# A second MLP whose first product is a one-level Strassen scheme on spans of 1024 tokens

## The chip, the cores and the metric

The kernel runs on one core of one Trainium2 chip. The metric is the device time of one execution in microseconds. The inputs and outputs are float32; the matrix products are made of pairs of float32r words, as told below.

## What is computed

Two steps of attention, then a gated MLP, then a second MLP without a gate. The change is in the second MLP. The reference, cut to that:

```python
def reference(**kwargs):
    attn_out = _attn_ref(...)                 # [8, 8, 576, 64]
    x = attn_out.transpose(0, 2, 1, 3).reshape(4608, 512)
    x = _moe_ref(x=x, ...)                    # gated MLP, 512 -> 1536 -> 512
    return _moe2_ref(x=x, ...)

def _moe2_ref(x, w_in, w_out):                # x [4608, 512]
    h = x @ w_in                              # w_in [512, 2048]
    g = h * (1.0 / (1.0 + np.exp(-1.702 * h)))
    return (g @ w_out).astype(np.float32)     # w_out [2048, 512]
```

The weights reach the kernel as pairs of 32-bit words, from which it builds float32 values on the chip.

## The kernel before

**Splitting.** Every operand of a large product is split into a float32r part h and a float32r rest l, and a product is three matmuls, h·h, h·l and l·h. A 512-deep product of a 128-row block thus takes 4 x 3 = 12 matmuls.

**The first MLP** (`mlp1`) runs in four units of two batches, 12 steps of 128 features each; attention of the next unit is woven into it, a stage at a time, by the driver loop at the end. `prods` multiplies weights with the packed attention values, `gateval` makes gate and value, `project` the output, which is summed in SBUF (`acc`) and written to DRAM (`x2_d`) as the second MLP's input. TensorE's results go through five PSUM buffers (pool `mm`); ACT, DVE and POOL empty them.

**Conversion.** `convert` turns one raw block of 128x512 word pairs into the two parts: an Abs on ACT, four bit operations on DVE (lines 116 to 119, with a buffer `between` in PSUM while the first MLP runs), a copy on ACT and a subtraction on POOL. The first MLP's weights are 36 such blocks, the second's 32.

**The second MLP** (`mlp2`). `early` runs beside the last unit of the first MLP: it converts nine of the sixteen 128-feature blocks of `w_in2` and `w_out2`, keeps three in SBUF and writes six to DRAM, and prepares the first tile of x. `main` then takes nine tiles of 512 tokens, and in each the sixteen feature blocks: `up(t, f)` makes 12 matmuls of 128x512 into one of four PSUM buffers, ACT applies the gelu, DVE splits the result (lines 903, 904); `down(t, f)` runs two blocks later and makes 4 x 3 matmuls of 128x512 that accumulate in four PSUM banks over all sixteen blocks, emptied once a tile. The remaining blocks are loaded and converted beside the first tile; from then on all weights lie in SBUF.

**Order.** The program is written in the order of its generators, and a scheduler with its own time model then orders the instructions of each engine; SP issues nearly all DMAs, in order. The stretches named below: attention and the first MLP up to 916 us, the second MLP from 916 us to the end.

## Time and profile before

| | |
|---|---|
| median of 3 runs | 1716.48 us (1715.28 to 1719.35) |
| span of the profiled execution | 1715.8 us |
| TensorE busy | 1686.7 us (98%) |
| VectorE (DVE), ScalarE (ACT), GpSimd (POOL) busy | 884.1, 677.0, 506.6 us |
| first matmul of the second MLP | 916.39 us |
| read from and written to DRAM | 138.41 and 44.04 MB |

The page's time is its span, from the first to the last instruction of one execution; the median of the runs is 0.7 us above it. A matmul's row has its modelled length, longer than the step from one start to the next, since matmuls are pipelined: the pace is read from starts. PEld is the load of the stationary operand, which overlaps matmuls.

### The profile page before, as it was taken

What the parts mean: (1) busy time and instruction counts of PE and PEld (TensorE: products, weight loads), DVE (VectorE), ACT (ScalarE), POOL (GpSimd) and SP (SyncE); (2) the same over time, 40 slices, a digit from 0 to 9 for tenths busy, and PEclk for the clock granted to TensorE, in tenths of its full rate; (3) what the DMA queues carried; (4) which work ended last, traced back from release to release, by engine and by line L of the source; (5) the groups of instructions that cost most, each with busy time, mean ns of one, the idle gap of its engine ahead of it and who ended that gap; (6) DMA issues with size and microseconds to landing.
All of it is one profiled execution on the core that took longest, in us unless ns stands there. A gap on an engine that the chain in (4) does not pass through costs nothing.

```text
span 1715.8 us, 24557 instructions
## 1 busy us (share of the span) xinstructions
PE 1686.7 (98%) x9360; PEld 1493.8 (87%) x9360; DVE 884.1 (52%) x1778; ACT 677.0 (39%) x1489; POOL 506.6 (30%) x515
## 2 busy tenths in 40 slices
PE   7899999999999999999999999999999999999999
PEld 5699998999999999999998888888888888888887
DVE  6789988657666566678884542212222222222221
ACT  5677776555555555555653321111111111110111
POOL 2357877544554355444662200000000000000000
PEclk9999999999999999999999999999999999999999
DMA  9666755543425443365666220101010101000000
GB/s 262 164 173 192 204 167 198 174 143 130 143 88 174 143 131 112 104 210 209 216 215 252 89 71 1 50 0 50 0 50 0 50 0 50 0 25 1 17 9 25
DMA packets 151909, 184.05 MB, mean 107 GB/s; under 512 B 87024, under 2 KB 123888, under 8 KB 144880
## 3 DMA queue, kind: packets, MB, share of 16 engines
q1 hardware_dynamic: 151504, 181.96, 33.5%
q8 instruction: 74, 1.21, 0.3%
q10 hardware_dynamic: 288, 0.52, 0.1%
q14 instruction: 43, 0.35, 0.1%
HBM read 138.41 MB, written 44.04 MB: 106 GB/s over the span
## 4 chain that ended last, share of the span: by engine, by line
PE 90%; DVE 3%; DMA 2%; ACT 2%; POOL 1%; SPq 1%; issue 1%; POOLq 0%; ACTq 0%; DVEq 0%
PE ps_up L897 23%; PE ps_dn L916 23%; PE ps_o L721 16%; PE ps_g L690 15%; PE ps_w L657 3%; PE ps_at L288 3%; PE ps_at L333 2%; PE ps_at L277 2%; PE ps_at L421 2%; DMA vn<-in_v_dram 1%; SPq L163 1%; DVE Wl L662 1%; PE ps_at L321 0%; POOL Hl L707 0%; DVE between L116 0%
## 5 line engine op out<-in xcount | busy, mean ns | idle before, releaser
L897 PE MATMUL ps_up<-xh,wi 128*128 128x512 f32 x1152 | 380.7, 393 | 0.7 <-DVE acc L731 0.7
L916 PE MATMUL ps_dn<-wo,gh 128*128 128x512 f32 x1152 | 356.5, 391 | 0.0
L903 DVE CAST gh<-gf 128x512 fp32r<-128x512 f32 x144 | 61.5, 427 | 514.3 <-ACT gf L900 508.9
L900 ACT ACTIVATE gf<-ps_up 128x512 f32<-128x512 f32 x144 | 86.2, 599 | 605.0 <-PE ps_up L897 586.2
L721 PE MATMUL ps_o<-Hh,wo 128*128 128x384 f32 x1152 | 323.1, 340 | 1.7 <-ACT Hh L706 1.2
L897 PEld LDWEIGHTS ps_up<-xh,wi 128*128 128x128 f32 x1152 | 216.2, 188 | 50.3 <-issue 1.0
L916 PEld LDWEIGHTS ps_dn<-wo,gh 128*128 128x128 f32 x1152 | 216.2, 188 | 47.9
L690 PE MATMUL ps_g<-Aqh,Wh 128*128 128x288 f32 x768 | 233.3, 304 | 4.1 <-ACT add L734 1.4
L690 PE MATMUL ps_g<-Aql,Wh 128*128 128x288 f32 x768 | 226.1, 295 | 0.0
L897 PE MATMUL ps_up<-xl,wi 128*128 128x512 f32 x576 | 225.8, 392 | 0.0
L690 PE MATMUL ps_g<-Aqh,Wl 128*128 128x288 f32 x768 | 225.5, 295 | 0.0
L916 PE MATMUL ps_dn<-wo,gl 128*128 128x512 f32 x576 | 224.4, 391 | 0.0
L721 PEld LDWEIGHTS ps_o<-Hh,wo 128*128 128x128 f32 x1152 | 210.7, 189 | 5.4 <-ACT Hh L706 1.9
L721 PE MATMUL ps_o<-Hl,wo 128*128 128x384 f32 x576 | 194.6, 339 | 1.1 <-POOL Hl L707 1.0
L707 POOL TENSOR_TENSOR Hl<-th,Hh 128x576 fp32r<-128x576 f32 x96 | 137.3, 1431 | 157.8 <-ACT Hh L706 155.9
L662 DVE TENSOR_TENSOR Wl<-ps_w,Wh 64x512 fp32r<-64x512 f32 x192 | 131.8, 687 | 71.9 <-ACT Wh L661 69.1
L736 POOL TENSOR_TENSOR acc<-acc,add 128x384 f32<-128x384 f32 x135 | 136.5, 1022 | 74.2 <-ACT add L734 72.2
L690 PEld LDWEIGHTS ps_g<-Aqh,Wh 128*128 128x128 f32 x768 | 144.0, 188 | 9.8 <-ACT add L734 1.6
L661 ACT CAST Wh<-ps_w 64x512 fp32r<-64x512 f32 x192 | 111.6, 581 | 83.2 <-PE ps_w L657 59.3
L690 PEld LDWEIGHTS ps_g<-Aql,Wh 128*128 128x128 f32 x768 | 144.3, 188 | 0.0
L690 PEld LDWEIGHTS ps_g<-Aqh,Wl 128*128 128x128 f32 x768 | 143.9, 188 | 0.0
L916 PEld LDWEIGHTS ps_dn<-wo,gl 128*128 128x128 f32 x576 | 108.1, 188 | 24.7
(154 smaller groups left out, 2506.9 us busy)
## 6 DMA issues: line engine op xcount, KB each, us to landing
wg<-wg SPq DMA_DIRECT2D x48, 1024.0 KB, 5.3
wo<-wo SPq DMA_DIRECT2D x48, 512.0 KB, 4.1
raw<-in_moe_w_out_dram SPq DMA_DIRECT2D x28, 512.0 KB, 4.0
x<-acc SPq DMA_DIRECT2D x32, 288.0 KB, 2.7
out_dram<-ob SPq DMA_DIRECT2D x34, 256.0 KB, 2.1
vn<-in_v_dram SPq DMA_DIRECT2D x16, 512.0 KB, 6.6
qn<-in_q_dram SPq DMA_DIRECT2D x64, 128.0 KB, 5.2
raw<-in_moe_w_in_dram SPq DMA_DIRECT2D x16, 512.0 KB, 3.8
```

The costliest lines, as they stand in the source:

```text
L288: nc.tensor.matmul(ps, x[:, a], y[:, a, span(e)], start=n == 0, stop=n == len(todo) - 1)
L657: last = nc.tensor.matmul(ps[:, a], st[:, i], mv[:, i], start=n == 0, stop=n == 2)
L661: nc.scalar.copy(Wh[rows, :, g], src)
L662: nc.vector.tensor_sub(Wl[rows, :, g], src, fl(Wh[rows, :, g]))
L690: nc.tensor.matmul(ps, st[:, o, g, c * P : (c + 1) * P], mv[:, g, cols], start=n == 0, stop=n == 3 * NG - 1)
L707: nc.gpsimd.tensor_sub(Hl, th, fl(Hh))
L721: nc.tensor.matmul(ps, st[:, m * P : (m + 1) * P], mv[:, cols], start=n == 0, stop=n == 3 * len(ss) - 1)
L736: nc.gpsimd.tensor_add(a, a, t)
L897: nc.tensor.matmul(ps, st[:, i], mv[:, i], start=n == 0, stop=n == 3 * NM - 1)
L900: nc.scalar.activation(gf, ps, AF.Gelu_apprx_sigmoid)
L903: nc.vector.tensor_copy(gh, gf)
L916: nc.tensor.matmul(pacc[r], st[:, r * P : (r + 1) * P], mv, start=f == 0 and n == 0, stop=f == NF2 - 1 and n == 2,)
```

## The change

The first product of the second MLP works on spans of 1024 tokens (four, and a last one of 512) and on pairs of feature blocks. A span's x is four quarters: b11 and b21 are the first and the second half of the depth for the first 512 tokens, b12 and b22 for the second 512. A pair's weights are four blocks a11 to a22. Instead of the eight block products there are seven, of sums and differences of blocks (`blocks`, `moving`); each is 2 x 3 = 6 matmuls, so a unit of one pair and one span has 42 of them and, with the second product, 90. In the last span they have 256 columns. The results are combined on DVE from four PSUM banks, one buffer each (`up`), with three products accumulated onto banks that already hold one.

The second product (`down`) no longer accumulates over the feature blocks in PSUM: for each pair and each 128 tokens six matmuls go to one of four banks, and DVE adds the bank to an accumulator in SBUF (`acc`; ACT copies it for the first pair).

All weights of the second MLP are converted during the first MLP once its own are done (`weights`, a step each 4.3 us of planned matmul time), with the sums of blocks formed and split there, and written to DRAM (`wi2_d`, `wo2_d`). `main` loads 1.8 MB (`wi`, two buffers) and 1.0 MB (`wo`, three buffers) for each pair and span, in alternating order of the pairs, so that the pair at a turn is kept. The first pair's blocks are loaded into the conversion buffers (`first_w`). x of the first span is prepared during the last unit of the first MLP (`first_x`), later spans during the last pair of the span before (`prepare`).

```diff
-    NKEPT = 3
-    NEARLY = 6
     MMB = 5
-    NTT = NT // TT
+    NP2 = NF2 // 2
+    TH = 512
+    WHOLE = NT // (2 * TH)
+    spans = [(i * 2 * TH, TH) for i in range(WHOLE)]
+    if NT % (2 * TH):
+        spans.append((WHOLE * 2 * TH, NT % (2 * TH) // 2))
+    SECOND = 4300.0
...
+    wi2_d = [dram.tile([P, 7, 2, 2, P], F32, name=f"wi2_{p}") for p in range(NP2)]
+    wo2_d = [dram.tile([P, 2, 2, DM], F32, name=f"wo2_{p}") for p in range(NP2)]
...
+        blocks = "s1 s2 s4 s3 a11 a12 a22".split()
+        moving = {"a11": "b11", "a12": "b21", "s4": "b22", "a22": "t4", "s1": "t1", "s2": "t2", "s3": "t3"}
...
+        def weights(banks):
+            for p in range(NP2):
+                ws = []
+                for h in range(2):
+                    r = raw_tile()
+                    nc.sync.dma_start(
+                        r.rearrange("p (i f) t -> p i f t", f=2 * P),
+                        w_in2[2 * h * P : 2 * (h + 1) * P, 2 * p * P : 2 * (p + 1) * P].rearrange(
+                            "(i p) f t -> p i f t", p=P
+                        ),
+                    )
+                    yield
+                    w = words(cv, r, DM, banks())
+                    ws.append(fl(w).rearrange("p (k i f) -> p i k f", k=2, f=P))
...
+                sums = cv.tile([P, 2, 2, 2, P], F32, tag="raw", name="sums", bufs=RAWS)
+                s1, s2, s4, s3 = (sums[:, i, j] for i in range(2) for j in range(2))
+                nc.gpsimd.tensor_add(s1, a21, a22)
+                nc.vector.tensor_sub(s3, a11, a21)
+                nc.vector.tensor_sub(s2, s1, a11)
+                nc.vector.tensor_sub(s4, a12, s2)
+                yield
+                for i in range(2):
+                    t = stage()
+                    nc.scalar.copy(t[:, :, 0], sums[:, i])
+                    nc.gpsimd.tensor_sub(t[:, :, 1], sums[:, i], fl(t[:, :, 0]))
+                    nc.sync.dma_start(wi2_d[p][:, 2 * i : 2 * i + 2], fl(t))
...
+                for f in range(2):
+                    r = raw_tile()
+                    nc.sync.dma_start(r, w_out2[(2 * p + f) * P : (2 * p + f + 1) * P])
+                    yield
+                    w = fl(words(cv, r, DM, banks()))
+                    t = cv.tile([P, 2, DM], F32R, tag="raw", name="stage", bufs=RAWS)
+                    nc.scalar.copy(t[:, 0], w)
+                    nc.gpsimd.tensor_sub(t[:, 1], w, fl(t[:, 0]))
+                    nc.sync.dma_start(wo2_d[p][:, f], fl(t))
...
-        def up(t, f):
-            xh, xl, _ = xt[t]
-            ih, il = wi[f]
-            ps = pools["pm"].tile([P, TT], F32, tag="up", name="ps_up")
-            n = 0
-            for i in range(NM):
-                for st, mv in ((ih, xh), (ih, xl), (il, xh)):
-                    nc.tensor.matmul(ps, st[:, i], mv[:, i], start=n == 0, stop=n == 3 * NM - 1)
-                    n += 1
-            gf = pools["sp"].tile([P, TT], F32, tag="gf", name="gf", bufs=2)
-            nc.scalar.activation(gf, ps, AF.Gelu_apprx_sigmoid)
-            gh = pools["sp"].tile([P, TT], F32R, tag="gh", name="gh", bufs=3)
-            gl = pools["sp"].tile([P, TT], F32R, tag="gl", name="gl", bufs=3)
-            nc.vector.tensor_copy(gh, gf)
-            nc.vector.tensor_sub(gl, gf, fl(gh))
-            gs[t, f] = gh, gl
...
-        def down(t, f):
-            gh, gl = gs.pop((t, f))
-            oh, ol = wo[f]
-            for r in range(TT // P):
-                if f == 0:
-                    pacc[r] = pools["pa"].tile([P, DM], F32, tag=f"dn{r}", name=f"ps_dn{r}")
-                for n, (st, mv) in enumerate(((gh, oh), (gh, ol), (gl, oh))):
-                    nc.tensor.matmul(
-                        pacc[r],
-                        st[:, r * P : (r + 1) * P],
-                        mv,
-                        start=f == 0 and n == 0,
-                        stop=f == NF2 - 1 and n == 2,
-                    )
-                if f == NF2 - 1:
...
+        def first_w():
+            t = [stage(), stage(), stage(), cv.tile([P, 1, 2, 2, P], F32R, tag="w", name="stage1", bufs=2)]
+            for i, x in enumerate(t):
+                nc.sync.dma_start(fl(x), wi2_d[0][:, 2 * i : 2 * i + x.shape[1]])
+            wi[0] = {q: t[i // 2][:, i % 2] for i, q in enumerate(blocks)}
...
+            def load_wi(n):
+                if n < len(seq) and seq[n][1] not in wi:
+                    p = seq[n][1]
+                    t = wp.tile([P, 7, 2, 2, P], F32R, tag="wi", name="wi", bufs=2)
+                    nc.sync.dma_start(fl(t), wi2_d[p])
+                    wi[p] = {q: t[:, i] for i, q in enumerate(blocks)}
...
+            def prepare(s, q):
+
+                if s == len(spans):
+                    return
+                n = spans[s][1]
+                b11, b12, b21, b22 = (xr[x] for x in ("b11", "b12", "b21", "b22"))
+                if q == "t2":
+                    xr[q] = spare()[:, :, :n]
+                    nc.vector.tensor_sub(xr[q], b22, b11)
+                source = {"t1": "b11", "t3": "b12", "t4": "b21"}.get(q, q)
+                split_x(q, xr[source], nc.gpsimd if q in ("b11", "b21", "b22") else nc.vector, n)
+                if q == "b11":
+                    nc.vector.tensor_sub(b11, b12, b11)
+                    nc.vector.tensor_sub(b12, b22, b12)
+                elif q == "b21":
+                    nc.vector.tensor_sub(b21, b21, xr["t2"])
...
+                def product(a, b, go_on=False):
+                    if not go_on:
+                        bank[b] = pm.tile([P, TH], F32, tag=f"up{b}", name="ps_up", bufs=1)[:, :n]
+                    wt, x, c = w[a], xb[moving[a]], 0
+                    for k in range(2):
+                        for y, z in ((0, 0), (0, 1), (1, 0)):
+                            nc.tensor.matmul(
+                                bank[b], wt[:, y, k], x[:, z, k], start=c == 0 and not go_on, stop=c == 5, skip_group_check=go_on
+                            )
+                            c += 1
+                    if last:
+                        prepare(s + 1, moving[a])
...
+                product("a11", 1)
+                p1 = temp("p1")
+                nc.scalar.copy(p1, bank[1])
                 yield
...
+                product("s2", 6)
+                u2 = temp("u2")
+                nc.vector.tensor_add(u2, p1, bank[6])
+                yield
+                product("s1", 5)
+                v5 = temp("v5")
+                nc.vector.tensor_add(v5, u2, bank[5])
+                yield
+                product("s3", 7)
+                c = temp("gf", 4)
+                nc.vector.tensor_add(c, v5, bank[7])
+                gelu(c, c, idx, 1, 1, n, nc.gpsimd)
+                yield
+                product("a12", 1, True)
+                gelu(temp("gf", 4), bank[1], idx, 0, 0, n, nc.gpsimd)
+                yield
+                product("s4", 5, True)
+                c = temp("gf", 4)
+                nc.vector.tensor_add(c, u2, bank[5])
+                gelu(c, c, idx, 0, 1, n, nc.gpsimd)
+                yield
+                product("a22", 7, True)
+                c = temp("gf", 4)
+                nc.vector.tensor_add(c, u2, bank[7])
+                gelu(c, c, idx, 1, 0, n, nc.vector)
+                yield
+
+            def gelu(gf, src, idx, i, k, n, engine):
+                nc.scalar.activation(gf, src, AF.Gelu_apprx_sigmoid)
+                gh, gl = (sp.tile([P, TH], F32R, tag=f"g{x}", name=f"g{x}", bufs=8)[:, :n] for x in "hl")
+                nc.vector.tensor_copy(gh, gf)
+                engine.tensor_sub(gl, gf, fl(gh))
+                g[idx, i, k] = gh, gl
...
+                for k in (1, 0):
+                    for r in range(per):
+                        ps = pa.tile([P, DM], F32, tag="dn", name="ps_dn", bufs=4)
+                        c = 0
+                        for i in range(2):
+                            gh, gl = g[idx, i, k]
+                            for st, y in ((gh, 0), (gh, 1), (gl, 0)):
+                                nc.tensor.matmul(
+                                    ps, st[:, r * P : (r + 1) * P], w[:, i, y], start=c == 0, stop=c == 5
+                                )
+                                c += 1
+                        m = k * per + r
+                        if first:
+                            acc[m] = sp.tile([P, DM], F32, tag=f"acc{m}", name="acc2", bufs=1)
+                            nc.scalar.copy(acc[m], ps)
+                        else:
+                            nc.vector.tensor_add(acc[m], acc[m], ps)
+                        if last:
+                            at0 = t0 + m * P
+                            nc.sync.dma_start(out[at0 : at0 + P, :], acc[m])
...
+            for idx, (s, p) in enumerate(seq):
+                ups = up(idx)
+                for _ in ups:
+                    next(behind_, None)
+                for _ in behind_:
+                    pass
+                nxt = [q for _, q in seq[idx + 1 : idx + 2]]
+                if idx and seq[idx - 1][1] not in (p, *nxt):
+                    wo.pop(seq[idx - 1][1], None)
+                if p not in nxt:
+                    wi.pop(p)
+                load_wi(idx + 2)
+                load_wo(idx + 2)
+                if idx and seq[idx - 1][0] != s:
+                    load_x(s + 1)
+                behind_ = down(idx)
...
+                    if finished():
+                        ready += what
+                        while ready >= SECOND:
+                            ready -= SECOND
+                            next(converting, None)
+            for _ in (*ahead, *converting):
                 pass
+            first_w()
```

TensorE in the middle of the second MLP. Before, `up` and `down` of one 512-token tile alternate (xh and xl are the parts of x, gh and gl those of the gelu's result):

```order
L897 MATMUL ps_up<-xh,wi_11814 128x512 x2
L897 MATMUL ps_up<-xl,wi_11814 128x512
L897 MATMUL ps_up<-xh,wi_11814 128x512
L916 MATMUL ps_dn_11887<-wo_11778,gh 128x512 x2
L916 MATMUL ps_dn_11887<-wo_11778,gl 128x512
L916 MATMUL ps_dn_11891<-wo_11778,gh 128x512 x2
L916 MATMUL ps_dn_11891<-wo_11778,gl 128x512
```

and now, where x_t and x_b are the seven moving operands and each product is six matmuls in a row:

```order
L999 MATMUL ps_up<-x_t_10160,wi 128x512 x6
L1062 MATMUL ps_dn<-wo_12819,gh 128x512 x2
L1062 MATMUL ps_dn<-wo_12819,gl 128x512
L1062 MATMUL ps_dn<-wo_12819,gh 128x512 x2
L1062 MATMUL ps_dn<-wo_12819,gl 128x512
L999 MATMUL ps_up<-x_b_10171,wi 128x512 x6
L1062 MATMUL ps_dn<-wo_12819,gh 128x512 x2
L1062 MATMUL ps_dn<-wo_12819,gl 128x512
```

Each block of the second product now ends after six matmuls, and its bank is emptied before it is used again.

DVE in the first MLP, where attention of a later unit is woven in. Before (Wl, kTl, acc and m are evictions of the first MLP and of attention):

```order
L662 TENSOR_TENSOR Wl<-ps_w,Wh 64x2x256
L402 STREAM_TRANSPOSE AT_4115<-t_4512 128x576
L662 TENSOR_TENSOR Wl<-ps_w,Wh 64x2x256
L144 TENSOR_TENSOR kTl<-ps_at,kTh 128x320
L728 COPY acc_4560<-ps_o 128x384
L662 TENSOR_TENSOR Wl<-ps_w,Wh 64x2x256
L728 COPY acc_4560<-ps_o 128x384 x2
L298 TENSOR_REDUCE m<-ps_at 128x1
L662 TENSOR_TENSOR Wl<-ps_w,Wh 64x2x256
```

and now, with the four operations of one conversion (raw_4565 is the block of word pairs):

```order
L119 TENSOR_SCALAR between<-w 128x512
L413 STREAM_TRANSPOSE AT_4148<-t_4563 128x576
L673 TENSOR_TENSOR Wl<-ps_w,Wh 64x2x256
L120 TENSOR_SCALAR between<-between 128x512
L155 TENSOR_TENSOR kTl<-ps_at,kTh 128x256
L739 COPY acc_4613<-ps_o 128x384
L155 TENSOR_TENSOR kTl<-ps_at,kTh 128x320
L121 SCALAR_TENSOR_TENSOR between<-raw_4565,between 128x512
L739 COPY acc_4613<-ps_o 128x384
L673 TENSOR_TENSOR Wl<-ps_w,Wh 64x2x256
L739 COPY acc_4613<-ps_o 128x384
```

The conversion's operations stand between the evictions, and the buffer `between` is held over them.

DVE at a turn from one token tile (before) or span (now) to the next. Before, one group splits the next x, and two banks of `down` are copied there by DVE:

```order
L903 CAST gh<-gf 128x512
L904 TENSOR_TENSOR gl<-gf,gh 128x512
L825 TENSOR_TENSOR xl<-xf,xh 128x512 x4
L903 CAST gh<-gf 128x512
L904 TENSOR_TENSOR gl<-gf,gh 128x512
L925 COPY ob<-ps_dn_12533 128x512
L903 CAST gh<-gf 128x512
```

and now, where u, v and gf are sums of product banks, xr the raw quarters of the next x, and x_t its split parts:

```order
L1071 TENSOR_TENSOR acc_12241<-acc_12241,ps_dn 128x512
L1015 TENSOR_TENSOR u_13145<-p_13123,ps_up 128x512
L978 TENSOR_TENSOR xr<-xr 128x1024
L1071 TENSOR_TENSOR acc_12259<-acc_12259,ps_dn 128x512
L979 TENSOR_TENSOR xr<-xr 128x1024
L974 TENSOR_TENSOR spare<-xr 128x1024
L1019 TENSOR_TENSOR v_13165<-u_13145,ps_up 128x512
L896 TENSOR_TENSOR x_t_13162<-xr,x_t_13162 128x1024
L1071 TENSOR_TENSOR acc_12277<-acc_12277,ps_dn 128x512
L1023 TENSOR_TENSOR gf<-v_13165,ps_up 128x512
L896 TENSOR_TENSOR x_t_13142<-spare,x_t_13142 128x1024
L1071 TENSOR_TENSOR acc_12300<-acc_12300,ps_dn 128x512
```

The eight subtractions of 1024 columns for the next span stand between the additions that empty TensorE's banks; five of them are seen here.

## Rows read from the trace of the kernel before

**Rows 1.** The page's busy line: us, share of the span, instructions.

```profile
PE 1686.7 (98%) x9360; PEld 1493.8 (87%) x9360; DVE 884.1 (52%) x1778; ACT 677.0 (39%) x1489; POOL 506.6 (30%) x515
```

**Rows 2.** The page's chain of work that ended last, by line.

```profile
PE ps_up L897 23%; PE ps_dn L916 23%; PE ps_o L721 16%; PE ps_g L690 15%; PE ps_w L657 3%; PE ps_at L288 3%; PE ps_at L333 2%; PE ps_at L277 2%; PE ps_at L421 2%; DMA vn<-in_v_dram 1%; SPq L163 1%; DVE Wl L662 1%; PE ps_at L321 0%; POOL Hl L707 0%; DVE between L116 0%
```

**Rows 3.** Stretches: busy us of PE, PEld, DVE, ACT, POOL; clock; DMA share; GB/s.

```profile
200.00:320.00 120.00, 116.14 (x778) 110.35 (x779) 95.11 (x199) 78.90 (x182) 82.86 (x83) 0.99 0.57 183
320.00:760.00 440.00, 440.00 (x3040) 427.97 (x3040) 287.63 (x615) 243.52 (x575) 212.21 (x219) 1.00 0.44 140
760.00:916.00 156.00, 154.00 (x1021) 150.66 (x1019) 121.68 (x224) 89.80 (x175) 87.34 (x72) 1.00 0.58 201
```

**Rows 4.** Costliest groups of the page: busy us, mean ns, idle before and releaser.

```profile
L897 PE MATMUL ps_up<-xh,wi 128*128 128x512 f32 x1152 | 380.7, 393 | 0.7 <-DVE acc L731 0.7
L900 ACT ACTIVATE gf<-ps_up 128x512 f32<-128x512 f32 x144 | 86.2, 599 | 605.0 <-PE ps_up L897 586.2
L897 PEld LDWEIGHTS ps_up<-xh,wi 128*128 128x128 f32 x1152 | 216.2, 188 | 50.3 <-issue 1.0
```

**Rows 5.** The chain in order of time: start us, us, what.

```profile
916.39 10.77 PE ps_up L897 x46
927.16 2.80 PE ps_dn L916 x12
...
1148.65 2.80 PE ps_up L897 x12
...
1703.43 8.21 PE ps_dn L916 x36
```

**Rows 6.** The timeline of TensorE, 256-column matmuls of attention: start us, modelled us.

```profile
479.77 0.28 PE L333 MATMUL ps_at<-vh,aTl 128*128 128x256 f32 x1
479.89 0.28 PE L333 MATMUL ps_at<-vh,aTh 128*128 128x256 f32 x1
```

**Rows 7.** DVE's groups by shape, from 916 us on, then before 916 us.

```profile
L904 DVE TENSOR_TENSOR gl<-gf,gh 128x512 fp32r<-128x512 f32 x144 | 99.5, 692 | 14.1 <-DVE gh L903 0.5
L903 DVE CAST gh<-gf 128x512 fp32r<-128x512 f32 x144 | 61.5, 427 | 514.3 <-ACT gf L900 508.9 <-PE ps_dn L916 5.3
L825 DVE TENSOR_TENSOR xl<-xf,xh 128x512 fp32r<-128x512 f32 x32 | 20.5, 702 | 3.5 <-ACT xh L824 3.5
...
L118 DVE SCALAR_TENSOR_TENSOR between<-raw,between 128x512 int32<-128x512 int32 x54 | 37.0, 686 | 0.4
L674 DVE TENSOR_TENSOR Aql<-AT,Aqh 128x576 fp32r<-128x576 f32 x16 | 13.0, 834 | 0.8 <-ACT Aqh L673 0.6
```

**Rows 8.** POOL's groups by shape, whole span.

```profile
L121 POOL TENSOR_TENSOR wo<-w,wo 128x512 fp32r<-128x512 f32 x22 | 28.4, 1291 | 58.2 <-ACT wo L120 58.2
L235 POOL TENSOR_TENSOR vl<-vn,vh 128x1024 fp32r<-128x1024 f32 x12 | 28.8, 2403 | 13.6 <-ACT vh L232 10.4 <-DMA qn<-in_q_dram 3.2
```

**Rows 9.** Waits of TensorE from 760 to 916: us in total, times, longest.

```profile
PE ps_g L690 <- DVE th L700: 0.5, 1, 0.5
PE ps_o L721 <- ACT add L734: 0.2, 1, 0.2
```

**Rows 10.** The timeline where the second MLP begins.

```profile
916.39 0.47 PE L897 MATMUL ps_up<-xh,wi 128*128 128x512 f32 x1 [0.74 <-DVE acc L731]
...
918.48 0.32 SPq L944 DMA_DIRECT2D wi<-w  x1
918.51 0.62 ACT L120 CAST wi<-w 128x512 fp32r<-128x512 f32 x1 [5.40 <-DMA x<-acc]
```

**Rows 11.** DMA of 918 to 938 in 40 slices; loads, KB each, us to landing.

```profile
GB/s 0 0 57 188 229 115 270 377 410 426 361 319 295 369 434 426 352 336 393 426 410 410 426 451 393 401 393 418 426 410 418 401 434 401 410 399 331 329 347 347
...
wi<-w SPq DMA_DIRECT2D x6, 512.0 KB, 9.2
...
wg<-wg SPq DMA_DIRECT2D x48, 1024.0 KB, 5.3
```

**Rows 12.** The timeline at the end: the last store's issue.

```profile
1712.28 0.34 ACTq L926 DMA_DIRECT2D out_dram<-ob  x1
```

More of the change, by code (lines that the diff above doesn't have):

```diff
@@ L1025, in tile_pack_attention__then__two_mlps @@
             u, ahead = 0, None
+            sources = [mm]
+            between = lambda: sources[-1]
+            weights, first_x, first_w, second = mlp2(cv)
+            converting, ready = weights(between), 0.0
             every = EVERY / len(todo)
```

249 lines of the change are left out of this document (129 added, 120 removed).

## The prediction

> **What bounds the kernel now.** I read the busy shares first: TensorE is busy 98% of the span [rows 1], and the chain that ended last is TensorE almost throughout, the two products of the second MLP alone 46% of it [rows 2]. Then the stretches [rows 3], all at full granted clock (2.4 GHz): of the 440 us from 320 to 760 TensorE idles none, of 200 to 320 it idles 3.9 us, of 760 to 916 2.0 us. A busy TensorE can hide slow issue, so I took its pace from the chain in order of time [rows 5]: twelve 512-column matmuls take 2.80 us at 927, where weights are converted and loaded beside them, and as long at 1148, where nothing else runs. From 916.39 to 1703.43 + 8.21 = 1711.64 lie 9 tiles x 16 x 24 = 3456 matmuls, so one costs 795.25 / 3456 = 0.2301 us, with no gap worth a term. So time is gained only by fewer or shorter matmuls, and lost only where TensorE is made to wait.
>
> **The matmuls removed.** The second product keeps its count: 36 blocks of 128 tokens x 8 pairs x 6 = 1728, all of 512 columns, as before. The first had 1728. Now four spans of 1024 tokens x 8 pairs x 42 = 1344 have 512 columns, and the last span (512 tokens) has 8 x 42 = 336 of 256 columns. Matmuls of 128x256 with a fresh 128x128 load each start 0.12 us apart [rows 6]. So 384 x 0.2301 = 88.4 us go and 336 x 0.12 = 40.3 us come: **-48.1 us**, all on the path, since the pace does not depend on what the other engines do [rows 5]. The Trainium skill (TensorE: Matmul & The Clock Gate, Back-to-back issue gap) gives a lone warm matmul N / 2.4 + 2.5 ns, thus an estimated 216 and 109 ns; by these the term would be 384 x 0.216 - 336 x 0.109 = 46 us. The same section's sustained 131 ns at 512 columns would make the 384 matmuls worth 50 us instead of 88. The rows agree with neither (2.80 us for twelve), so the trace decides.
>
> **More conversion under the first MLP.** Before, 18 of the 32 conversions of the second MLP's weights run before 916 (the 54 of [rows 7] less 36 for the first MLP), the rest beside the first token tile, where TensorE never waits. Now all 32 run between about 275 and 880, plus 24 sums on DVE, the splits of seven blocks instead of four, and six 128x1024 subtractions of x. DVE gains 14 x 4 x 0.69 = 38 us, 24 x 0.35 = 8 us (half a 128x512 subtraction) and 6 x 1.40 = 8 us (two of them) [rows 7]: about 55 us on top of 409 in 596 us [rows 3], from 69% to 78%. Each conversion also holds one of the five PSUM buffers that the first MLP rotates through, and its raw block is asked for only one step ahead, so a late landing stands at the head of ACT's queue, with the evictions behind it that TensorE needs. The stretch 760 to 916 is already that mixture at 78% DVE and idles 2.0 of 156 us, on results of DVE and ACT among others [rows 9]; over 596 us that is 7.6, so 5.6 more than now. Ends: evenly spread it could cost nothing and free the 2.0 us; at the density of 200 to 320 (3.9 of 120 us, with attention beside it) it costs 19.2 - 2.0 = 17. I take **+5**, by the row with the same DVE share. On SP's queue the stores of converted blocks wait for POOL ahead of loads of the first MLP's weights; these are issued a pair of steps or more ahead and land in about 5 us [rows 11], so I price that at nothing; without that cover it is such a landing each.
>
> **The turn to the second MLP.** Now TensorE waits 0.7 us there [rows 10]. The first seven products need blocks loaded earlier into the conversion buffers and x prepared earlier, so they start alike and last 42 x 0.23 = 9.7 us, to about 926. The second pair's 1.8 MB are issued behind the last x stores and wait, as the loads there did, until those landed: 918.5 [rows 10]. A 1 MB load took 5.3 us, at the some 400 GB/s of that stretch 2.6 of transfer and 2.7 beside it; 1.8 MB so take 4.6 + 2.7 = 7.3 and land near 925.8; the queued 512 KB loads took 9.2 us [rows 11], which would make it 927.7, 1.7 late. Take **+0.5**, ends 0 and 1.7. ACT's first eviction (with its gelus queued behind) waits for the same stores, but its bank is needed only four products later.
>
> **The steady unit** (one pair, 90 matmuls, 20.7 us). DVE has five sums of a bank, eight additions into the SBUF accumulator, four casts, one subtraction: 13 x 0.70 + 4 x 0.43 + 0.69 = 11.5 us, ACT five passes of 0.6, POOL three of 1.3 [rows 4, 7, 8]. The longest chain, from the sixth product over DVE, ACT, DVE and POOL to the next unit's first block, is 0.7 + 0.6 + 0.4 + 1.3 and one addition ahead, about 4 us, against 7 us of matmuls placed between them; a bank comes round after 5 us or more. So **0**. Weights stream 2.9 MB a unit, 140 GB/s against the 400 shown [rows 11]. In the last span a unit is 42 x 0.12 + 24 x 0.23 = 10.6 us and needs 273 GB/s; a pair's 1.8 MB has about 9 us from its freed buffer to its first product and takes 7.3, or 9.9 with the pair's other 1 MB just ahead of it. Take **+2**, ends 0 and 6 x 1.
>
> **The four span boundaries.** The next x is split while the last pair runs: eight 128x1024 DVE subtractions, 8 x 1.40 = 11.2 us, on the 11.5: 22.7 us in a unit of 20.7 [rows 7]. The order puts three products of the new span ahead of the second product, 4 us of cover, and the next unit's first additions are ACT copies. I take 0.75 each, **+3**; ends 0 and 4 x 3. The Trainium skill (SBUF — State Buffer, Who interferes with whom) says that a DVE instruction with two SBUF inputs and a POOL instruction that reads SBUF exclude each other for a whole instruction; the rows show at most a 7% longer DVE subtraction where POOL is busy (834 ns for 576 columns against 692 x 576 / 512 = 778) [rows 7]. By the rows that adds 0.8 us of DVE time a boundary; by the rule it is a rival below.
>
> **Tail.** Before, DVE and ACT copied in turn and ACT issued the last store [rows 12]; now two additions of 0.7 follow each other on DVE: **+0.7**, ends 0 and 1.5.
>
> **Sum.** -48.1 + 5 + 0.5 + 2 + 3 + 0.7 = -36.9 on the profiled 1715.8 us: 1678.9. The median of the runs, 1716.5, is 0.7 above that span, so **1679.6 us**. All low ends give -50.1 (1666.4), all high ends -9.9 (1706.6).
>
> **Rivals.**
> - Nothing waits: every cover holds and the conversions cost no more than now, 1666 to 1670. For it: 440 us without idle [rows 3]. Against: DVE rises to 78%, where TensorE waited before. 13%.
> - Conversions stall the first MLP: at the rate of 200 to 320 or twice that, +17 to +36 instead of +5, 1692 to 1711. For it: raw blocks are fetched one step ahead. Against: the density there was several times higher. 15%.
> - Slower: the evictions of the products come onto the path. The four product banks have one buffer each; where the chain copy, sum, sum, gelu, cast, split (0.6 + 0.7 + 0.7 + 0.6 + 0.4 + 1.3 = 4.3 us) is not covered, a unit is that much longer. From 48.1 / 36 = 1.3 us a full unit (two halves for the last span's) the gain is gone; with half the chain, 2.15 x 36 = 77, the time is 1679.6 + 77 = 1757. Against: the order leaves 7 us where 4 are needed, and DVE is at 55%. 7%.
> - DVE and POOL exclude each other at the boundaries: POOL's 3 x 2.40 + 3 x 1.30 = 11.1 us a boundary [rows 8] come onto DVE, 44 us instead of 3: 1721, slower by 0.2%. Against: the 7% above. 1%. The rule of the Trainium skill (SBUF — State Buffer, Who interferes with whom) is this mechanism.
> - The change doesn't shorten what it says: 256-column matmuls run at the pace of the weight loads, whose rows are 188 ns long [rows 4]; +336 x 0.068 = 23, 1702. Against: the same loads stand between the 0.12 us starts of [rows 6]. 3%.
>
> **Chances.** The forecast (1671 to 1691) holds 61%. For 8 in 10 the range takes in the rival without waits from its lower end and two thirds of the conversion rival: 1666 to 1702. What a measurement of this kernel tells from no change is about 0.2% (3.4 us); the time is below that bound in all cases but the evictions' and the boundaries', 8 in 100, of which I put 2 within it: faster 0.92, same 0.02, slower 0.06.
>
> **What would show it.** The stretch from the first product to the last matmul should be 747 us plus at most some 8 of waits, 1680 matmuls of the first product on the page. TensorE idle between 320 and the turn: 5 to 8 us in small waits on DVE and ACT; more, or waits of 2 us on a raw block, say the conversion rival. A wait for the second pair's weights at the turn, or 6 of them in the last span, says the streaming was mis-sized. Waits of TensorE on DVE in every unit say the eviction rival. The forecast is wrong if the pace of 512-column matmuls leaves 0.23 us, or if the 256-column ones are not near 0.12.

## The result: 1.5% faster, two thirds of the forecast gain

| | before | after |
|---|---|---|
| median of the runs beside each other | 1716.4 us | 1692.19 us (1690.34 to 1693.33, 4 runs) |
| ratio, 95% interval | | 0.9852 [0.9838, 0.9866] |
| span of the profiled execution | 1715.8 us | 1691.4 us |
| end of each unit of the first MLP (first store of its sums) | 309.64, 523.22, 736.23, 909.69 | 313.84, 526.96, 752.77, 927.13 |
| first matmul of the second MLP | 916.39 | 933.79 |
| from there to the end of the span | 799.4 us | 757.6 us |

The forecast was 1679.6 us; the time lies 12.6 us above it, inside the range. The last two lines of the table say where the difference lies. The second MLP became 41.8 us shorter, against 41.9 in the forecast (the sum without the 5 us of the conversions); that these agree so closely is luck, as is shown at the end. The first MLP became 17.4 us longer, against 5. Of these 17.4 the third unit alone has 12.8 (225.8 us from store to store instead of 213.0).

The page of the changed kernel, busy line, answers to [rows 1]:

```profile
PE 1649.5 (98%) x9312; PEld 1465.1 (87%) x9312; DVE 1148.6 (68%) x2154; ACT 730.7 (43%) x1586; POOL 719.3 (43%) x680
```

Its stretches (start and end, length; busy us and instructions of PE, PEld, DVE, ACT, POOL; granted clock; DMA share; GB/s), to be held against [rows 3]:

```profile
320.00:730.00 410.00, 409.60 (x2829) 397.76 (x2828) 318.82 (x662) 253.57 (x601) 246.05 (x256) 1.00 0.62 200
730.00:740.00 10.00, 8.47 (x56) 7.84 (x55) 8.91 (x14) 8.59 (x14) 7.59 (x4) 1.00 0.47 165
740.00:745.00 5.00, 1.50 (x8) 0.86 (x6) 5.00 (x3) 1.42 (x2) 3.83 (x3) 0.93 0.00 0
745.00:750.00 5.00, 3.03 (x10) 2.56 (x11) 4.66 (x6) 1.63 (x2) 5.00 (x3) 0.50 0.02 3
750.00:755.00 5.00, 5.00 (x19) 5.00 (x18) 3.43 (x6) 2.35 (x5) 3.89 (x3) 0.55 0.69 252
755.00:760.00 5.00, 5.00 (x33) 5.00 (x32) 3.19 (x6) 2.92 (x6) 4.34 (x4) 1.00 1.00 335
760.00:775.00 15.00, 14.64 (x108) 14.23 (x107) 12.45 (x25) 9.28 (x17) 7.86 (x5) 1.00 0.90 312
775.00:780.00 5.00, 3.02 (x15) 2.57 (x14) 4.93 (x8) 1.33 (x4) 0.59 (x1) 0.84 0.35 105
```

The 410 us that carry most of the new conversions idle 0.4 us, with DVE busy at 78%. Most of the loss is one hole of some 20 us, at the end of the third unit. TensorE idles 7.0 us between 730 and 755, and from 745 to 755 its clock is granted at about half (1.2 GHz), so that the 8 busy us there do the work of some 4. Another 2.0 us are lost at 775 to 780. Together that is about 13 us. The longest waits of TensorE from 730 to 800 name DVE for 6.6 of their 9.0 us and ACT for the rest (us in total, times, longest):

```profile
PE ps_o L732 <- DVE th L709: 3.5, 2, 2.0
PE ps_o L732 <- ACT add L745: 2.4, 1, 2.4
PE ps_o L732 <- DVE acc L742: 2.0, 1, 2.0
PE ps_w L668 <- DVE Wl L673: 1.1, 1, 1.1
```

What DVE, and then POOL, do there is in their timelines (start us, us, line, operation, tiles, shapes):

```profile
737.20 0.89 DVE L685 TENSOR_TENSOR Aql<-AT,Aqh 128x576 fp32r<-128x576 f32 x1
738.37 3.06 DVE L910 TENSOR_TENSOR x_t<-x_t 128x1024 f32<-128x1024 f32 x1
741.35 0.74 DVE L685 TENSOR_TENSOR Aql<-AT,Aqh 128x576 fp32r<-128x576 f32 x1
742.01 3.38 DVE L896 TENSOR_TENSOR x_b<-x_t,x_b 128x1024 fp32r<-128x1024 f32 x1
745.32 0.54 DVE L742 TENSOR_TENSOR acc<-acc,ps_o 128x384 f32<-128x384 f32 x1
746.38 1.36 DVE L896 TENSOR_TENSOR x_t<-x_t,x_t 128x1024 fp32r<-128x1024 f32 x1
```

```profile
737.42 2.92 POOL L896 TENSOR_TENSOR x_b<-x_t,x_b 128x1024 fp32r<-128x1024 f32 x1
741.50 2.81 POOL L911 TENSOR_TENSOR x_t<-x_t,x_t 128x1024 f32<-128x1024 f32 x1 [1.17 <-DVE x_t L910]
744.27 2.39 POOL L718 TENSOR_TENSOR Hl<-th,Hh 128x576 fp32r<-128x576 f32 x1
```

Lines 896 to 924 are `first_x` and its `split_x`, the preparation of the first span's seven operands. The code asks for one step of it per piece of the last unit, but the program's scheduler set its instructions ahead of the third unit's last sums. There they meet the 128x576 subtractions of `scaled` (L685) and Wl (L673). A 128x1024 subtraction of two tiles in SBUF, which takes 1.2 to 1.4 us elsewhere, takes 3.06 and 3.38 us while POOL works. In front of what TensorE waits for stand 3 us here and 3 us there.

### The profile page after: what moved, and what is told of

It is laid out like the page before. It is cut to its first block, busy times and chain, and to the rows that moved or that the text cites. A ratio compares the mean times of both kernels' runs of the same rounds, so it can differ in the third digit from the quotient of the medians.

```text
span 1691.4 us, 25480 instructions
## 1 busy us (share of the span) xinstructions
PE 1649.5 (98%) x9312; PEld 1465.1 (87%) x9312; DVE 1148.6 (68%) x2154; ACT 730.7 (43%) x1586; POOL 719.3 (43%) x680
## 4 chain that ended last, share of the span: by engine, by line
PE 85%; DVE 5%; DMA 3%; ACT 2%; issue 2%; POOL 1%; SPq 1%; DVEq 0%; POOLq 0%; ACTq 0%
PE ps_dn L1062 23%; PE ps_up L999 21%; PE ps_o L732 16%; PE ps_g L701 13%; PE ps_w L668 3%; PE ps_at L299 2%; PE ps_at L344 2%; PE ps_at L288 2%; PE ps_at L432 1%; DMA raw<-in_moe_w_out_dram 1%; SPq L174 1%; DMA vn<-in_v_dram 1%; DVE Wl L673 1%; DVE th L709 1%; DVE th L711 1%
## 5 line engine op out<-in xcount | busy, mean ns | idle before, releaser
L1044 POOL TENSOR_TENSOR gl<-gf,gh 128x512 fp32r<-128x512 f32 (+1 forms) x120 | 148.3, 1237 | 529.8 <-DVE gh L1043 527.9
L1071 DVE TENSOR_TENSOR acc<-acc,ps_dn 128x512 f32<-128x512 f32 x252 | 172.4, 686 | 163.2 <-PE ps_dn L1062 161.9
L1041 ACT ACTIVATE gf<-gf 128x512 f32<-128x512 f32 (+1 forms) x120 | 70.8, 590 | 399.9 <-DVE gf L1023 245.6
L999 PE MATMUL ps_up<-x_t,wi 128*128 128x512 f32 (+1 forms) x936 | 224.9, 371 | 0.0
L999 PEld LDWEIGHTS ps_up<-x_t,wi 128*128 128x128 f32 x936 | 165.5, 188 | 34.3
L673 DVE TENSOR_TENSOR Wl<-ps_w,Wh 64x512 fp32r<-64x512 f32 x192 | 131.8, 687 | 68.8 <-ACT Wh L672 65.7
L999 PE MATMUL ps_up<-x_b,wi 128*128 128x512 f32 (+1 forms) x702 | 165.1, 372 | 0.4 <-ACT gf L1041 0.4
L999 PEld LDWEIGHTS ps_up<-x_b,wi 128*128 128x128 f32 x702 | 123.5, 188 | 26.4 <-issue 0.8
```

Of the source, the lines that this page charges most:

```text
L673: nc.vector.tensor_sub(Wl[rows, :, g], src, fl(Wh[rows, :, g]))
L999: nc.tensor.matmul(bank[b], wt[:, y, k], x[:, z, k], start=c == 0 and not go_on, stop=c == 5, skip_group_check=go_on)
L1041: nc.scalar.activation(gf, src, AF.Gelu_apprx_sigmoid)
L1044: engine.tensor_sub(gl, gf, fl(gh))
L1071: nc.vector.tensor_add(acc[m], acc[m], ps)
```

## The experiments

Two theories stood against each other, each with a part that could be tested alone. **A:** the clump of `first_x` at the turn of the third unit makes the hole, either because DVE and POOL keep each other out of SBUF (A1) or because of the sheer amount of work in DVE's queue (A2). **B:** the weight conversions beside the first MLP cost it, as the conversion rival had it. For the length of the first MLP the table takes the time from the first unit's store to the first matmul of the second MLP (606.8 us before, 620.0 in the changed kernel), since the first store itself comes anywhere between 308.9 us (e10) and 313.8 us (the changed kernel) where the order of the work up to it is the same. This time differs between executions too: e7, whose first MLP has the order of the changed kernel, took 622.7. So differences of less than some 3 us in that column say nothing.

| run | that time | PE idle, 730 to 760 | clock there | time |
|---|---|---|---|---|
| changed kernel | 620.0 | 7.0 | 0.83 | 1692.2 |
| e1, preparation spread | 610.3 | 1.0 | 1.00 | 1684.1 |
| e2, all of it on DVE | 618.6 | 5.9 | 0.89 | 1690.9 |
| e3, all of it on POOL | 617.1 | 4.7 | 0.89 | 1689.9 |
| e9, conversions held back there | 618.9, and a wait of 9.1 in front of the first matmul | 7.5 | 0.72 | 1725.6 |
| e6, conversions denser | 635.9 | 8.5 | 0.91 | 1707.7 |

In e6 the third unit's first store is at 768.6, so its turn lies mostly behind the stretch of the two middle columns. e2, e3, e4, e6, e7 and e9 were run once each, the others four or five times.

### e1: the preparation spread over the last unit

```diff
-                        nc.vector.scalar_tensor_tensor(t, t, 1.0, ps, op0=ALU.add, op1=ALU.mult)
+                        marked["DVE"] = nc.vector.scalar_tensor_tensor(t, t, 1.0, ps, op0=ALU.add, op1=ALU.mult)
...
                     if ahead is not None and u == NU - 1:
-                        next(ahead, None)
+                        if late % 16 == 0 and late >= 0:
+                            with behind("DVE"), behind("ACT"), behind("POOL"):
+                                next(ahead, None)
+                        late += 1
```

`behind` ties what is issued to the latest marked instruction of that engine (the evictions in `gateval`; those of ACT and POOL are marked in the same way), so the scheduler can't pull it ahead.

> The changed kernel with one difference: the eleven steps that prepare the first span's operands are tied behind the running work of the last unit of the first MLP, one step to 16 of its pieces, so that they lie some 15 us apart instead of all between 733 and 775 us. Theory A (the 12.8 us that the changed kernel loses between 730 and 780 us, against a forecast of 5 for all of the conversions, come from these steps standing together in front of the subtractions and evictions that TensorE waits for): the hole goes, TensorE is busy at least 29 of 30 us in 730 to 760, the end of the third unit's sums falls from 752.8 to 740-742, and the whole takes 1677 to 1682 us, ratio to before 0.977 to 0.980. Theory B (the load of the weight conversions on VectorE is what costs): the conversions are unchanged, so the loss is only spread; 1688 to 1693, ratio 0.983 to 0.986.

1684.14 us, ratio 0.9805 [0.9788, 0.9822] where the changed kernel has 0.9852. The stretch that held the hole:

```profile
730.00:760.00 30.00, 28.98 (x190) 27.50 (x190) 25.08 (x46) 16.96 (x35) 12.80 (x12) 1.00 0.73 264
```

The third unit ends at 741.82, as A said, and 9.7 of the 13.2 us by which the first MLP had become longer from that first store on are gone. The profiled span, 1680.9, lies where A had the time; the median lies 2 us above A's range. From 760 to 920 TensorE idles 4.5 us instead of 2.9: a little of the cost was only moved. The 3.5 us that are left are what TensorE idles more than before: 0.3 from 320 to 730, 1.0 from 730 to 760 and 2.1 from 760 to 920.

### e2 and e3: the preparation on one engine

```diff
-            split_x("b11", b11, nc.gpsimd)
+            split_x("b11", b11, nc.vector)
```

and so for all five wide subtractions that POOL had (e2), or the other way for DVE's six (e3).

> The changed kernel with the five wide subtractions of the first span's preparation that GpSimd does given to VectorE, which then does all eleven; the place in the order stays at the turn of the third unit. Theory A1 (VectorE's 128x1024 operations with both inputs in SBUF last 3.1 and 3.4 us instead of 1.2 to 1.4 because GpSimd works in SBUF at the same time): the wide ones fall to 1.2 to 1.4 us each except beside GpSimd's other work, the eleven take about 15 us together where the six took 13.4, and TensorE's idle time in 730 to 760 stays at or below 7 us: 1687 to 1693. Theory A2 (it is the amount of work put into VectorE's queue there, not the stretching): five more operations in that queue add 5 to 8 us to the hole: 1695 to 1700.

> The changed kernel with all eleven wide subtractions of the first span's preparation on GpSimd. Eleven of 2.4 us are 26 us of GpSimd there. Theory A1 (stretching): VectorE has no wide operation left there, but its 128x576 subtractions (0.75 us alone, up to 2.1 beside GpSimd) and GpSimd's own Hl and sums queue behind 26 us: half of the hole at least stays, now as waits for GpSimd; 1686 to 1695. Theory A2 (amount of work in VectorE's queue): VectorE is relieved of all 13.4 us, the waits for VectorE go, 1679 to 1684.

1690.85 and 1689.89 us, both in the range of A1 and not of A2. That is no gain either: the changed kernel's own runs go down to 1690.34. In e2 most wide subtractions of DVE are back at their own length (count; minimum, median and maximum in ns, by line and tiles):

```profile
L896 DVE TENSOR_TENSOR x_b<-x_t,x_b x3: 1210/1210/2424, 734.0 to 742.2; 128x1024 fp32r<-128x1024 f32 x3
L896 DVE TENSOR_TENSOR x_t<-x_t,x_t x3: 1206/1207/1216, 746.3 to 771.8; 128x1024 fp32r<-128x1024 f32 x3
```

All eleven together take DVE some 16.3 us, 1.5 each. The six of the changed kernel take 12.4 (3.06, 3.38, 1.36, 1.23, 1.22 and 2.16; the expectation's 13.4 is a slip), 2.1 each, of which about 4.9 us are stretching. In e3, where DVE has no wide subtraction left, the exclusion is still there: of the 128x576 subtractions of `scaled`, 0.75 us each alone, two take 2.15 and 2.57 us beside POOL (the second one's row):

```profile
738.26 2.57 DVE L685 TENSOR_TENSOR Aql<-AT,Aqh 128x576 fp32r<-128x576 f32 x1
```

The hole stays in both kernels, 5.9 and 4.7 us of idle time. In e2, with most of the stretching gone, the work itself still stands in the way; in e3 it is the exclusion, and POOL's own queue, that can. Neither A1 nor A2 alone is the cause, and how the loss divides between them was not separated; only moving the work in time (e1) closed the hole.

### e4: the price of the exclusion

> None of the kernel's computation is in this one: it only runs repeated operations of two engines on constant tiles, first each alone, then side by side, and writes a constant to the output. It prices what the forecast took as 7 per cent. Theory A1 (the two engines stretch each other where both of VectorE's inputs or its one input lie in SBUF): the 128x1024 subtraction on VectorE goes from 1.2 us alone to 2.5 to 3.5 beside GpSimd's 128x1024 subtractions, the 128x512 rounding copy from 0.41 to about 1.2, and the 128x512 addition with one input in PSUM stays at 0.69; GpSimd's own go from 2.4 to 2.8 to 3.5. Rival (what was seen at 740 us was some other contention, DMA writes or the semaphores): beside GpSimd everything stays within 10 per cent of its time alone.

First alone: the timeline of DVE, and one line of POOL.

```profile
7.86 10.04 DVE L60 TENSOR_TENSOR dr<-d,d 128x1024 fp32r<-128x1024 f32 x8 [1.79 <-ACT d L77]
18.40 5.78 DVE L63 TENSOR_TENSOR dr<-d,d 128x512 fp32r<-128x512 f32 x8 [0.50 <-ACT d L77]
24.68 5.74 DVE L66 TENSOR_TENSOR do<-d,ps 128x512 f32<-128x512 f32 x8 [0.50 <-ACT d L77]
30.91 3.66 DVE L69 CAST dr<-d 128x512 fp32r<-128x512 f32 x8 [0.50 <-ACT d L77]
```

```profile
35.28 19.25 POOL L72 TENSOR_TENSOR pr<-p,p 128x1024 fp32r<-128x1024 f32 x8 [30.28 <-ACT d L76]
```

Then side by side: two rows of the timeline for the wide subtractions and two for the additions with an input in PSUM, and the groups of the stretch 141 to 160.4 for the casts (busy us, mean ns).

```profile
54.79 37.29 DVE L60 TENSOR_TENSOR dr<-d,d 128x1024 fp32r<-128x1024 f32 x12 [20.22 <-ACT d L75]
122.72 17.29 DVE L66 TENSOR_TENSOR do<-d,ps 128x512 f32<-128x512 f32 x24 [0.45 <-ACT d L75]
```

```profile
55.12 39.15 POOL L72 TENSOR_TENSOR pr<-p,p 128x1024 fp32r<-128x1024 f32 x12 [0.59 <-ACT p L78]
123.05 14.50 POOL L72 TENSOR_TENSOR pr<-p,p 128x1024 fp32r<-128x1024 f32 x6 [6.41 <-ACT p L78]
```

```profile
L69 DVE CAST dr<-d 128x512 fp32r<-128x512 f32 x8 | 19.6, 2444 | 0.3
L72 POOL TENSOR_TENSOR pr<-p,p 128x1024 fp32r<-128x1024 f32 x8 | 19.2, 2402 | 3.7 <-ACT p L78 3.2
```

| DVE beside POOL's 128x1024 subtraction (2.41 us alone) | alone | beside | POOL beside |
|---|---|---|---|
| subtraction 128x1024, both inputs in SBUF | 1.26 | 3.11 | 3.26 |
| addition 128x512, one input in PSUM | 0.72 | 0.72 | 2.42 |
| cast 128x512, SBUF to SBUF | 0.46 | 2.44 | 2.40 |

The rival (within 10%) fell, and A1 was too low for the cast: 2.44 us, not 1.2. A DVE instruction of these forms gets its turn once for each POOL instruction; the pair of wide subtractions takes 3.26 us where one after the other would take 3.67, and that with a cast 2.44 where it would be 2.87, so only some 0.4 us overlap. The form with an input in PSUM is not touched.

This is the rule of the Trainium skill (SBUF — State Buffer, Who interferes with whom): DVE instructions with two SBUF inputs, and casts and copies in the modes that take both ports, hold or wait for a port pair shared with GpSimd, and others don't. The forms agree with it here. Its "fully blocks" for a whole instruction agrees but for those 0.4 us.

### e5, e8, e10: what more there is to gain

e5 adds to e1 that two products of the first matrix and two blocks of the second take turns, instead of one and one:

```diff
-                for _ in ups:
-                    next(behind_, None)
+                for n, _ in enumerate(ups):
+                    if n % 2:
+                        next(behind_, None)
+                        next(behind_, None)
```

> The spread preparation of e1, and in the second MLP two products of the first matrix and then two blocks of the second in turn, instead of one and one. Everything computed is the same. In the changed kernel six matmuls of 128x512 take 1.39 to 1.40 us where the two products alternate (0.232 each), 24 of one kind in a row 5.46 us (0.2275): 0.025 us for each change from one product to the other, 14 changes in a unit of 90. Theory C (a change of product costs TensorE that much): the steady unit goes from 20.85 to 20.70 us and the 32 units of the whole spans give 5 us: 1677 to 1681, ratio 0.976 to 0.979. Rival: the 0.025 us belongs to every accumulation group of six, whatever stands next to it, or two products in a row wait for their evictions: unit at 20.85 or above, 1683 to 1690.

1680.73 us, ratio 0.9777 [0.9760, 0.9793], the lowest median of all and inside theory C's range, but not for the reason given: the steady unit takes 20.83 us instead of 20.85, and 20.70 was expected. Its interval overlaps that of e1, and 0.02 us in 32 units are 0.6 us. The chain of e5 in order of time shows why theory C fell:

```profile
959.94 2.76 PE ps_dn L1062 x12
962.70 2.80 PE ps_up L999 x12
965.50 2.76 PE ps_dn L1062 x12
```

Twelve of the first product take 2.80 us, twelve of the second 2.76, also without a change between sixes.

> As the spread and paired version, with all eleven wide subtractions of the spread preparation on VectorE, so that GpSimd's 2.4 us subtractions no longer stand against VectorE's operations with SBUF inputs. Theory A1 (the exclusion is what is left of the cost): TensorE's idle time from 760 to 920 us falls from 4.5 to 3 us or less, 1 to 3 us faster than the spread and paired version. Rival (a wide operation in VectorE's queue costs as much as one in GpSimd's, once they are spread): within 1 us of it, or slower by up to 2.

1681.32 us, ratio 0.9793 [0.9771, 0.9814]: the same as e5. TensorE idles 4.3 us from 760 to 920 where e5 idles 4.8. Once the preparation was spread, no difference showed by which engine did it; the rival held.

e10 is e1 with each cast and subtraction in two halves.

> The spread preparation of e1 with each of its casts and subtractions cut into two of 128x512. If VectorE and GpSimd take turns by whole instructions, as the priced pairs showed (one VectorE instruction for each 2.4 us of GpSimd's), a 128x512 one on GpSimd holds VectorE for 1.3 us instead: TensorE's idle time from 760 to 920 falls from 6.2 (e1: 37.92 of 40 and 117.61 of 120 busy, so 4.5) to 3, and the whole is 1 to 3 us faster than e1: ratio 0.978 to 0.980. Rival (the waits that are left come from the number of instructions ahead in VectorE's and ScalarE's queues): no change, or 1 to 2 us slower, ratio 0.980 to 0.982.

1684.46 us, ratio 0.9811 [0.9798, 0.9825], no gain, and 5.2 us idle from 760 to 920 instead of 4.5 (the 6.2 in the expectation is a slip): the rival held. Shorter turns at SBUF gave nothing here; that the number of instructions in the queues is the reason was not shown.

### e6: the conversions denser

```diff
-    SECOND = 4300.0
+    SECOND = 3200.0
```

> The changed kernel with the weight conversions of the second MLP a third denser (one step to 3.2 us of matmuls instead of 4.3), so that they end about where the last unit begins. Theory A (conversions beside the first MLP cost next to nothing, only the first span's preparation at the turn of the third unit does): TensorE stays over 99.5 per cent busy between 320 and 730, the hole at 730 to 760 stays within 2 us of its 7, the last unit is 1 to 3 us shorter: 1686 to 1692. Theory B (the conversions' load on VectorE costs): a third more of it in 320 to 730 opens waits there, 10 us and more: 1695 to 1705.

1707.71 us, 15 more than the changed kernel: theory A fell, and B's waits came, though the time lies 3 us above its range. In one stretch of the first MLP, of e6 and then of the changed kernel:

```profile
310.00:730.00 420.00, 409.53 (x2774) 392.25 (x2773) 332.83 (x689) 257.08 (x606) 256.61 (x265) 1.00 0.66 212
```

```profile
310.00:730.00 420.00, 419.60 (x2890) 407.12 (x2889) 325.77 (x674) 258.04 (x610) 251.46 (x261) 1.00 0.61 200
```

DVE's share rises from 78% to 79% only, but TensorE idles 10.5 us instead of 0.4. So the conversions are not free as such: they are hidden at one step in 4.3 us of matmuls and no longer at one in 3.2. At the turn the waits grow too, one of 4.8 us on the eviction th (L709), where the longest wait of the changed kernel is 2.4. The order of the attention's work moved as well in this kernel, and how much of the 10.5 us is due to that was not separated.

### e7: an eighth product

```diff
                 product("a11", 1)
+                product("a11", 1)
...
```

The second call computes the same bank again, and the operands' preparation waits for the second (the lines left out).

> The changed kernel with the product a11 x b11 computed twice in every pair of every span, so eight products in place of seven: 32 x 6 = 192 matmuls of 512 columns and 8 x 6 = 48 of 256 more, and nothing else. This undoes the saving of the seventh part alone. Theory (the second MLP is bound by the count of matmuls at 0.23 and 0.12 us, with the rest hidden): +192 x 0.2301 + 48 x 0.12 = 49.9 us, 1739 to 1744, slower than before. Rival (part of the unit's time is not TensorE's: evictions or weights): +35 or less, below 1728.

1749.50 us, 57 more. The steady unit is 22.25 us instead of 20.85: 1.40 for six matmuls, and in the last span 11.10 instead of 10.43. That is 32 x 1.40 + 8 x 0.67 = 50.2 us, as expected. The profiled span is 56.0 us longer (1747.4); of the other 5.8 us, 2.6 are in the first MLP, where the order is that of the changed kernel, and 3.2 in the second. Of these, 1.3 are at its start, where the first bank's eviction now starts a product later and TensorE waits for what follows on it (0.72 and 0.66 us in two rows of the timeline), and 0.64 at each of the three boundaries between whole spans, whose units take 22.89 us and where TensorE waits for x_t (L896), prepared a product later. So the time came out 5 us above what was expected, for these reasons; the rival, hidden time, fell. The second MLP is paid in matmuls.

### e9: the conversions held back at the turn

```diff
+                if what == "attention" and u == NU - 2:
+                    hold = 40
...
+                    if u == NU - 1 and hold:
+                        hold -= 1
-                    if finished():
+                    if finished() and not hold:
```

> The changed kernel with the weight conversions held back from the last step of the third unit until the last unit has run 40 pieces, some 730 to 780 us; the first span's preparation stays where it was, all together, and the held conversions move into the last unit. It tells the two apart at one place. Theory A (the clump of preparation alone makes the hole): the third unit still ends at 749 to 753 us and TensorE is still idle 6 to 8 us in 730 to 760. Theory B (it is clump plus conversions): the third unit ends at 741 to 746 and the idle time is 3 us or less. The whole is 1688 to 1696 by A, 1680 to 1687 by B, where the last unit doesn't give it back.

At the turn A holds: without a conversion in it, the stretch idles as long, and its clock is lower still; the third unit's first store is at 755.75, 3 us behind what A gave.

```profile
730.00:745.00 15.00, 10.05 (x46) 8.09 (x44) 13.46 (x16) 9.76 (x15) 11.93 (x6) 0.80 0.31 113
745.00:760.00 15.00, 12.50 (x50) 10.84 (x50) 11.37 (x13) 6.50 (x11) 9.79 (x6) 0.63 0.35 130
```

The whole, 1725.6 us, lies far outside both expectations. The held conversions now end at the very end of the first MLP, and the first pair's weights are loaded into the buffers in which the conversions work (`first_w`). So these loads come late, the last behind loads of x in SP's queue at 953.5 us (897.2 in the changed kernel), and the second MLP waits for them, 9.1 us ahead of its first matmul and 20.5 ahead of its nineteenth (TensorE's waits from 920 to 990, a stretch there, and the last load's issue):

```profile
PE ps_up L999 <- DMA stage<-wi: 29.6, 2, 20.5
920.00:970.00 50.00, 20.31 (x91) 17.40 (x89) 8.60 (x14) 4.99 (x10) 9.98 (x9) 0.70 0.80 294
953.54 0.32 SPq L934 DMA_DIRECT2D stage<-wi  x1
```

Conversions have a window with two ends: denser they stall the first MLP, later they stall the start of the second. The changed kernel's pace lies inside it; how much room it has on either side, these two points don't show.

## Why the forecast was right, and where it was not

- **The matmuls.** -48.1 forecast. Steady units take 20.85 us instead of 20.71: 32 x 0.14 = 4.5 us less gain; in the last span they take 10.43 instead of 10.56, 1 us more gain: -44.6. The count was right (e7). The pace was mis-sized by 0.7%: 0.2301 us was the mean of two paces. Before, 24 matmuls take 2.80 + 2.76 = 5.56 us in some stretches (those of [rows 5] are from such), and in others, as here, 5.44 (chain of the kernel before; the two kinds alternate, for some 50 to 110 us each):

```profile
1206.99 2.72 PE ps_dn L916 x12
...
1212.43 2.72 PE ps_dn L916 x12
1215.15 2.72 PE ps_up L897 x12
```

  The changed kernel has the slower one in every steady unit (90 matmuls at 0.2317). The prediction took two rows that happened to be at 2.80 as proof that the pace doesn't change. What sets it stays open: in the kernel before, DMA moved 1 GB/s both from 1105 to 1165 (slower) and from 1210 to 1265 (faster).
- **The 256-column matmuls.** 0.12 from [rows 6] against 0.11 (e7: 0.67 / 6). The rival of the weight loads' pace fell.
- **The boundaries.** +3 forecast, 0 measured: the three units around each take 62.5 us together from first product to first product, as three steady ones do. And yet the exclusion is there (DVE's timeline; the second row is two casts that take 0.41 each alone, the third is beside a wide subtraction of POOL):

```profile
1249.99 1.22 DVE L896 TENSOR_TENSOR x_t<-xr,x_t 128x1024 fp32r<-128x1024 f32 x1
1251.72 2.37 DVE L1043 CAST gh<-gf 128x512 fp32r<-128x512 f32 x2
1258.38 2.83 DVE L896 TENSOR_TENSOR x_t<-xr,x_t 128x1024 fp32r<-128x1024 f32 x1
```

```profile
1247.00:1267.00 20.00, 20.00 (x88) 16.18 (x88) 19.63 (x25) 7.11 (x10) 12.13 (x6) 1.00 0.52 157
```

  DVE is busy 19.63 of 20 us and TensorE idles none: the cover of 4 us of products and the copies on ACT were enough together; which of them mattered was not tested. The rival of the 1% named the right mechanism, and its place was wrong.
- **The rest of the second MLP** (turn +0.5, last span +2, tail +0.7) is 2.8 us together, but in other places: a wait of 0.4 us at the second pair, on ACT's gelu and not on the weights, one of 1.1 before the last products, on DVE's cast, and 0.5 us behind the last matmul. No wait on weights is seen in the last span. The steady unit's +0 held: no wait in any of them. So the second MLP as a whole came out at the forecast by luck: the matmuls gained 3.5 us less, and the boundaries' 3 us were not paid.
- **The conversions**, +5 spread evenly over 596 us in small waits: this is the step that failed. Evenly they cost 0.4 us in 410. The share of DVE by which the term was priced doesn't give the waits: at 78% TensorE idles 0.4 us of 410 in the changed kernel, at 79% 10.5 of 420 in e6. The six wide subtractions of `first_x` were added to DVE's load in the same term, as 6 x 1.40 = 8 us among 55; in truth they stand with POOL's five in one place, in front of the turn of a unit, and cost some 10 us there (e1 against the changed kernel). By the prediction's own signs, more than 8 us of idle time between 320 and the turn to the second MLP (here 10.3 by 920) would have meant the conversion rival; e1 and e9 show that it was the preparation of x. Of the 17.4 us of the first MLP, 9.7 go with the clump, and 3.5 stay from the first unit's store on when it is spread. The other 4.2 lie before that store: 1.5 of them are there ahead of any difference in the order, and 2.7 come at 303 to 309, where two subtractions of `scaled` take 2.24 us between four steps of a conversion:

```profile
304.48 2.24 DVE L685 TENSOR_TENSOR Aql<-AT,Aqh 128x576 fp32r<-128x576 f32 x2
```

- **The 7%.** The boundary part refused the exclusion on a mean of 834 ns in [rows 7]. The same 16 instructions of the kernel before, by minimum, median and maximum, show what the mean hid: thirteen ran at their own length, and three took 1.04, 1.05 and 1.53 us.

```profile
L674 DVE TENSOR_TENSOR Aql<-AT,Aqh x16: 728/750/1527, 72.6 to 733.6; 128x576 fp32r<-128x576 f32 x16
```

  Each of the three began while a 128x576 subtraction of POOL ran, and ended 0.61 us behind it. So the price stood in the trace of before (POOL's timeline, then DVE's):

```profile
296.71 1.45 POOL L707 TENSOR_TENSOR Hl<-th,Hh 128x576 fp32r<-128x576 f32 x1 [0.22 <-ACT Hh L706]
297.24 1.53 DVE L674 TENSOR_TENSOR Aql<-AT,Aqh 128x576 fp32r<-128x576 f32 x1
```

  A mean over cases of which few overlap POOL is no price of the overlap.

## What to carry to other kernels

Work that is off the path and has time should not only be counted as load: ask where the scheduler puts it, and tie it behind running work if it comes in one piece just where the other engines' queues are fullest (8 us here, from one edit). A price of contention is read from those instances of an instruction that overlap the other engine, or measured with two engines side by side, not from the mean of a group. A cover is worth what stands in the place: the same exclusion that cost nothing at the span boundaries, behind 4 us of queued products, was part of a hole of 13 us where TensorE had sums to wait for.

## What the runs showed of the hardware that was not expected

- A cast of 128x512 on DVE, 0.41 to 0.46 us alone, takes 2.44 us beside GpSimd's 128x1024 subtractions: it gets one turn for each (e4). At a boundary of the changed kernel two of them took 2.37 us together.
- A stretch of 10 us in which TensorE was busy 4.5 us (740 to 750) came with a granted clock of 0.50 and 0.55 from 745 to 755, though TensorE was busy throughout the last five of these: the hole costs about half as much again as its idle time.
- Matmuls of 128x512 follow each other at 0.2267 or at 0.2300 to 0.2333 us for long stretches of the same kernel, without a wait that the profile shows and at the same granted clock of 1.00.
